# First x tile by TensorE, key softmax sums without transposes, memory features in five chunks

## The chip, the cores and the metric

One core of a Trainium2 chip. The time is device microseconds of one execution of the whole kernel. TensorE is PE, VectorE DVE, ScalarE ACT, GpSimd POOL, SyncE SP. SP computes nothing here; it issues nearly all DMAs, in order.

## The reference, cut to what matters

Two attention layers over the same x, mixed by a gate. 2048 tokens, 640 features, 32 heads of 20.

```python
g = sigmoid((x * gate_w).sum(-1))                 # per token
# A: linear attention with softmax features
q, k, v = split(x @ wqkv)
phi(t) = concat(softmax(t @ w_phi), softmax(-(t @ w_phi)))    # over 20, per head
o = (phi(q) @ (phi(k).T @ v)) / (phi(q) @ phi(k).sum(tokens) + 1e-6)
a = o @ wo
# B: four segments of 512 tokens; causal softmax inside one, a memory of those before
q, k, v = x @ wq, x @ wk, x @ wv
f(t) = where(t > 0, t + 1, exp(t))
for s in range(4):
    a_dot = softmax(causal(q_s @ k_s.T / sqrt(20))) @ v_s
    a_mem = (f(q_s) @ M) / (f(q_s) @ z + 1e-6)
    o_s = sigmoid(beta) * a_mem + (1 - sigmoid(beta)) * a_dot
    M, z = M + f(k_s).T @ v_s, z + f(k_s).sum(tokens)
b = concat(o_s) @ wo
out = g * a + (1 - g) * b
```

## The kernel before

The program is first a list of operations, each with its engines, an assumed duration, what it reads and writes, and a priority (`pr`, smaller is sooner). A planner (`schedule`) then places them one by one: of those that can start about now it takes the one with the smallest `pr`, and for an operation that may run on two engines the engine that is free sooner. SBUF tiles come from small pools and PSUM banks from a common one, and an operation waits until its tile is free. The result is a fixed order for each of PE, ACT, DVE, POOL and SP, and `emit` writes it out with a semaphore wait in front of what needs one. On the chip each engine works through its list in order: whatever stands behind a waiting instruction waits too. The planner's durations are guesses written in the code (a transposing DMA of 640 columns holds SP for 1.0 us and lands 2.0 us later).

`setup` loads x transposed into `xT` in four tiles of 512 tokens, by DMA from SP (`xload`), the first one ahead of everything. Three weights come through ACT's queue, the others through SP's. Wq and Wk of B are loaded as they are (`stq`, `stk`) and copied into `WB` with columns in a new order (L655, L657): each of five chunks of 128 columns holds four heads of 20, each followed by 12 of the 240 columns of the last twelve heads. Wk and Wq of A are loaded transposed (`wkT`, `wqT`) and multiplied with w_phi on PE (`fuse`).

B, for each segment n: `b_proj` makes `qk` in five chunks (L722). The 12-column remainders are written to `scr` in memory and read back (`relw`, `relr`) as groups 5 to 7 of `qk`, so that there are eight groups of four heads, each head on its own 32 partitions. `b_step`, for each group: QK on PE (L854), exp on ACT (L864, L883), the causal mask on POOL (L869, one instruction per block of 128 keys), PV on PE (L909); there are two exp buffers. From segment 1 on PE also reads out the memory (L912) with `b_pq`'s features (L825, L826, L828, four parts of two groups), and `combine` (L932 to L958) divides, scales and adds on DVE. `b_mem`, after segments 0 to 2: eight DMA transposes of the keys (`kT`, into `pk`), features (L784, L786, L788), 32 matmuls (L798), and the sum masked to the four heads' own blocks (L811).

A, keys: `a_k` for each of 16 tiles of 128 tokens, spread among B's steps by `AK`: pkA and vA on PE (L996, L997), two exps of 640 columns into `E` (L1003). For the softmax sums per head, `spread` transposes `E` by two DMAs, PE multiplies the result with a head mask (Zk, L1017), DVE takes the reciprocal (L1022) and normalizes `E` (L1023); `spread` transposes the normalized `E` again, and DVE adds that up over tokens into `acc` (L1032). After four tiles `a_kv` multiplies `E` with v (L1055) and adds to `KVZacc` (L1066).

A, queries: `a_q` for each segment, placed by `AQ`. `final` (placed by `FI`) multiplies the transposed results of both layers with `Wo` and stores the output. Results of all segments but the last are transposed by DMA (`oTB`, `oTA`), those of the last by PE.

## Time and profile before

| | |
|---|---|
| median of 3 runs (lowest to highest) | 391.79 us (388.26 to 394.04) |
| the profiled execution, and its span | 390.8 us, 388.9 us |
| busy: PE, ACT, DVE, POOL | 323.3, 268.1, 222.4, 106.3 us |
| mean granted TensorE clock | 0.925 |
| DMA packets, bytes | 97721, 33.97 MB |

How to read it: the span is from the first to the last instruction, the profiled execution's own time is taken around it. Busy time of PE includes matmuls at the lower clock; the granted clock is 1 where PE has its full 2.4 GHz and 0.5 where it has 1.2. Issuing a DMA isn't counted as busy, so SP's load shows only in its timeline.

### The profile page before, as it was taken

Reading aid. Unit: us, or ns where it says so; the run is one execution under the profiler, and the core shown is the slowest. Engines: PE = TensorE matmul, PEld = TensorE weight load, DVE = VectorE, ACT = ScalarE, POOL = GpSimd, SP = SyncE. Lnnn points to the kernel's source line nnn. Section 1 sums busy time; section 2 is a strip of 40 time slices with the busy share of each in tenths; the row PEclk is TensorE's granted clock in tenths of the full one; section 3 lists DMA queues with packets and bytes.
Section 4 is the critical chain, followed back from the end, with each engine's and each line's share of the span. In section 5 each row is a group of like instructions: output and inputs, shape, how many; then the busy total and the mean of one; then the engine's idle time right before and its main releaser. Section 6 shows DMA issues by size and latency. Waiting matters only on the chain.

```text
span 388.9 us, 9141 instructions
## 1 busy us (share of the span) xinstructions
PE 323.3 (83%) x3892; PEld 184.5 (47%) x3892; DVE 222.4 (57%) x447; ACT 268.1 (69%) x349; POOL 106.3 (27%) x155
## 2 busy tenths in 40 slices
PE   0997477996977989879976889899999897996786
PEld 0344144464543554446543545466555544552563
DVE  2203237985627577477818896777455476335760
ACT  2458545975865885847885879978697789567532
POOL 8402210232320122312323352512233323224210
PEclk9999868999995998969996999999999999996699
DMA  9999766366453666853452882023233513210002
GB/s 176 259 202 190 140 96 104 63 85 92 88 92 76 98 117 106 133 101 54 76 99 42 201 136 52 3 45 70 76 35 35 92 47 32 55 52 1 2 2 69
DMA packets 97721, 33.97 MB, mean 87 GB/s; under 512 B 89809, under 2 KB 95761, under 8 KB 97681
## 3 DMA queue, kind: packets, MB, share of 16 engines
q1 hardware_dynamic: 95616, 30.89, 44.4%
q10 hardware_dynamic: 1968, 2.46, 2.5%
q8 instruction: 31, 0.51, 0.6%
q0 software_dynamic: 96, 0.04, 0.1%
q14 instruction: 10, 0.07, 0.1%
HBM read 6.92 MB, written 4.59 MB: 30 GB/s over the span
## 4 chain that ended last, share of the span: by engine, by line
PE 47%; SPq 15%; ACT 14%; DVE 11%; DMA 7%; issue 2%; POOL 2%
SPq L598 13%; PE ps L1210 9%; ACT expT L864 7%; PE ps L722 7%; PE ps L996 5%; PE ps L909 5%; PE ps L854 4%; DMA TT<-E 3%; PE ps L1109 3%; PE ps L1211 2%; DVE cb L955 2%; DMA wkT<-in_A_wqkv_dram 2%; PE ps L1170 2%; SPq L603 2%; POOL expT L869 2%
## 5 line engine op out<-in xcount | busy, mean ns | idle before, releaser
L869 POOL TENSOR_SCALAR_AFFINE_SELECT expT<-expT 128x512 bf16<-128x512 bf16 x128 | 89.9, 705 | 260.2 <-ACT expT L864 203.5
L864 ACT ACTIVATE expT<-ps 128x1024 bf16<-128x1024 f32 x128 | 123.5, 1025 | 24.5 <-PE ps L854 24.4
L722 PE MATMUL ps<-xT,WB 128*128 128x512 bf16 x200 | 55.3, 423 | 10.6 <-DMA xT<-in_A_x_dram 10.6
L909 PE MATMUL ps<-v1B,expT 128*128 128x21 bf16 x1280 | 43.4, 174 | 6.0 <-DVE oA L1179 2.3
L909 PEld LDWEIGHTS ps<-v1B,expT 128*128 128x128 bf16 x1280 | 39.7, 97 | 17.2 <-POOL expT L869 6.9
L883 ACT ACTIVATE expT<-ps 128x1024 bf16<-128x1024 f32 x32 | 32.8, 1026 | 19.1 <-PE ps L854 19.0
L854 PE MATMUL ps<-qk 20*128 20x384 bf16 (+3 forms) x512 | 36.4, 320 | 10.9 <-DVE cb L955 5.2
L722 PEld LDWEIGHTS ps<-xT,WB 128*128 128x128 bf16 x200 | 19.1, 105 | 34.9 <-issue 19.6
L996 PE MATMUL ps<-WkA,xT 128*128 128x512 bf16 x80 | 26.5, 417 | 2.5 <-ACT qk L706 1.4
L743 PE MATMUL ps<-WvB,xT 128*128 128x512 bf16 x80 | 25.1, 396 | 3.9 <-DVE vA L707 3.7
L1003 ACT ACTIVATE E<-ps 128x640 bf16<-128x640 f32 x32 | 22.8, 711 | 8.0 <-PE ps L997 7.6
L706 ACT ACTIVATE out<-ps 128x640 bf16<-128x640 f32 x16 | 11.3, 704 | 22.5 <-PE ps L1211 19.6
L996 PE MATMUL ps<-WvA,xT 128*128 128x512 bf16 x80 | 25.6, 405 | 1.0 <-ACT E L1003 0.4
L1210 PE MATMUL ps<-Wo,oTA 128*128 128x512 bf16 x80 | 24.8, 396 | 1.7 <-ACT expT L864 1.7
L854 PEld LDWEIGHTS ps<-qk 20*128 20x128 bf16 x512 | 10.5, 93 | 32.8 <-issue 10.1
L1032 DVE TENSOR_TENSOR acc<-acc,TT 128x640 bf16<-128x640 bf16 x31 | 16.8, 541 | 15.0 <-DMA TT<-E 14.5
L1109 PE MATMUL ps<-xT,WqA 128*128 128x512 bf16 x100 | 24.3, 380 | 1.1 <-DVE cb L955 1.0
L706 ACT ACTIVATE qk<-ps 128x512 bf16<-128x512 f32 x29 | 17.2, 602 | 11.0 <-PE ps L722 10.5
L1023 DVE TENSOR_TENSOR E<-E,z 128x1280 bf16<-128x1280 bf16 x16 | 24.1, 1508 | 0.6
L1114 ACT ACTIVATE ET<-ps 128x512 bf16<-128x512 f32 x40 | 23.1, 607 | 1.9 <-PE ps L1109 1.2
L1210 PE MATMUL ps<-Wo,oTB 128*128 128x512 bf16 x80 | 23.7, 383 | 0.0
L955 DVE TENSOR_TENSOR cb<-ps,cs 128x640 bf16<-128x640 f32 x24 | 19.8, 825 | 0.8
(124 smaller groups left out, 551.4 us busy)
## 6 DMA issues: line engine op xcount, KB each, us to landing
out_dram<-out SPq DMA_DIRECT2D x16, 160.0 KB, 3.8
scr<-qk SPq DMA_DIRECT2D x16, 120.0 KB
qk<-scr SPq DMA_DIRECT2D x16, 120.0 KB
TT<-E SPq DMA_TRANSPOSE x64, 2.7
stq<-in_B_wq_dram ACTq DMA_DIRECT2D x1, 800.0 KB, 4.8
stk<-in_B_wk_dram ACTq DMA_DIRECT2D x1, 800.0 KB, 6.8
WvB<-in_B_wv_dram ACTq DMA_DIRECT2D x1, 800.0 KB, 11.8
WvA<-in_A_wqkv_dram SPq DMA_DIRECT2D x1, 800.0 KB
```

Of the source, the lines that this page charges most:

```text
L598: return e.dma_start_transpose(o() if callable(o) else o, i() if callable(i) else i)
L706: return e.activation(o(), i(), ACT.Copy)
L722: r = e.matmul(self.pf(pt, 0, 0, LSEG), lhsT=self.WB[:, w, kc, 128 * c:128 * (c + 1)], rhs=xT[:, kc, LSEG * n:LSEG * (n + 1)], start=(kc = ...
L854: r = e.matmul(self.pf(pts[i][0], pts[i][1], c0, N), lhsT=qk[32 * i:32 * i + DH, g, 1, 128 * j:128 * (j + 1)], rhs=qk[32 * i:32 * i + DH, ...
L864: self.op("act", d_act(1024), lambda e, p=p, pt=pt: e.activation(ex[:, 2 * p:2 * p + 2, off:off + 512], self.pbanks(pt, 0, 2, 512), ACT.Ex ...
L869: self.op("pool", d_pool(n_el), lambda e: e.affine_select(view(), view(), pattern=pat, compare_op=ALU.is_ge, fill=0.0, base=0, channel_mul ...
L883: return e.activation(ex[:, :, 1024:1280].rearrange("p (k b) c -> p k b c", k=2), src, ACT.Exp, scale=scale)
L909: r = e.matmul(self.pf(ad, b, 84 * q2 + 21 * i, 21) if n else self.pf(ad, 0, 84 * qi + 21 * i, 21), lhsT=ex[:, i, c0:c0 + 128], rhs=vt[:, ...
L955: self.op("dve", d_dve(640, 1, True), lambda e: e.tensor_tensor(cb[:, :, :, :].rearrange("p b t (x d) -> p b (t x) d", d=DH), Uv()[:, :, : ...
L996: e.matmul(self.pf(pt, 0, 0, 512), lhsT=l, rhs=W[:, kc, 0:512], start=(kc == 0), stop=(kc == 4))
L1109: r = e.matmul(self.pf(pt, 0, 0, LSEG), lhsT=self.WqA[:, kc, 128 * c:128 * (c + 1)], rhs=xT[:, kc, LSEG * S:LSEG * (S + 1)], start=(kc == ...
L1210: e.matmul(self.pf(pt, 0, 0, 512), lhsT=l, rhs=self.Wo[:, c, 0:512], start=(c == 0), stop=(c == 9))
```

## The change

The first x tile is loaded as it is, in one plain DMA (`xr`, in the second exp buffer's place), transposed by 20 PE operations against the identity and evacuated by DVE or ACT. The weights that ACT issued are issued by SP after it, Wq and Wk in two pieces each, and the copies into `WB` go by pieces; the order of the other loads on SP is new. ACT starts with an exp on a zeroed tile. The two zeroing memsets of `qk` on POOL are gone.

The last twelve heads are regrouped (`head_of`), so that groups 5 to 7 hold heads 20 to 31 in order. The memory works on the five chunks instead of the eight groups: five key transposes, features of 5 x 128 columns, 40 matmuls with a bigger block mask `Mm` (built by 22 POOL selections); query features are made by chunk (five operations of 512 columns for four of 1024), and the read-out of a group whose heads lie in several chunks takes one matmul per chunk (`mem_parts`).

In `a_k` the sums per head are made from `E` itself: 640 pairs are added into fp32, then 320 pairs, both on POOL or DVE, then DVE reduces five columns to one and takes the reciprocal. The transposes for Zk, Zk itself and its PSUM bank are gone; the remaining transpose of a tile is one DMA of 1280 columns for two of 640.

Planner numbers are new: durations of transposes (1.28 us and 1.5 us to landing; 2.3 and 1.6 for the 1280), `AK`, `AQ`, `FI`, priorities of key transposes and features.

```diff
+XH = tuple(20 + 48 * c // DH for c in range(NCH))
 
 
 def head_of(g, i):
-    return 4 * g + i if g < 5 else 20 + 3 * i + (g - 5)
+    return 4 * g + i
 
...
-    AK = (1.0, 1.05)
-    AQ = (18.2, 4.4)
-    FI = 9.0
+    AK = (1.6, 0.996)
+    AQ = (17.6, 4.1)
+    FI = 8.5
...
-        self.p_pq = self.pool(3, 2048)
-        self.p_tmp = self.pool(2, 2048)
-        self.p_pk = self.pool(1, 8192)
+        self.p_pq = self.pool(7, 1024)
+        self.p_pk = self.pool(1, 5120)
+        self.p_tmp = self.pool(2, 1280)
...
-            return self.dma("sp", xT[:, :, sl], x2d[sl, :], W=[(xT, s)], pr=pr, transpose=True, name=f"x{s}", dur=dur, lat=1.5)
-        x0 = xload(0, -40, 4.0)
-        sq = self.dma("act", self.stq[:, :, :], wsrc(ins["B_wq"]), W=[(self.stq, "*")], pr=-40, lat=5.0, name="stq")
-        sk = self.dma("act", self.stk[:, :, :], wsrc(ins["B_wk"]), W=[(self.stk, "*")], pr=-39, lat=5.0, name="stk", after=[sq])
-        sv = self.dma("act", self.WvB[:, :, 0:D], wsrc(ins["B_wv"]), W=[(self.WvB, "w")], pr=-38, lat=7.0, name="WvB", after=[sq])
-        self.dma("sp", self.wkT[:, :, :], wqkv[0:D, D:2 * D], W=[(self.wkT, "*")], pr=-38, dur=5.0, lat=1.5, transpose=True, name="wkT", after=[sk])
-        self.dma("sp", self.WvA[:, :, :], wsrc(wqkv[:, 2 * D:3 * D]), W=[(self.WvA, "*")], pr=-37, lat=6.0, name="WvA", after=[sv])
-        for i in range(1, SEG):
-            xload(i, -37 + i, 3.4)
-        self.dma("sp", self.wqT[:, :, :], wqkv[0:D, 0:D], W=[(self.wqT, "*")], pr=-30, dur=5.8, lat=1.5, transpose=True, name="wqT")
+            return self.dma("sp", xT[:, :, sl], x2d[sl, :], W=[(xT, s)], pr=pr, transpose=True, name=f"x{s}", dur=dur, lat=3.0)
+        zf = self.zf
+        self.op("dve", 0.1, lambda e: e.memset(zf[:, :, :], 0.0), W=[(zf, "*")], pr=-60)
+        self.op("act", 1.5, lambda e: e.activation(zf[:, :, :], zf[:, :, :], ACT.Exp), W=[(zf, "*")], pr=-60)
+        xr = self.xr
+        self.dma("sp", xr[:, :, :], x2d[0:LSEG, :].rearrange("(t p) d -> p t d", p=128), W=[(xr, "*")], pr=-60, lat=3.2, name="xr")
+        for k, (st, w) in enumerate(((self.stq, "B_wq"), (self.stk, "B_wk"))):
+            for h, (k0, k1) in enumerate(((0, 3), (3, 5))):
+                self.dma("sp", st[:, k0:k1, :], wsrc(ins[w])[:, k0:k1, :], W=[(st, h)], pr=-59 + 2 * k + h, lat=4.6 + 2.0 * k + h, name="st")
+        self.dma("sp", self.WvB[:, :, 0:D], wsrc(ins["B_wv"]), W=[(self.WvB, "w")], pr=-54, lat=8.0, name="WvB")
+        self.dma("sp", self.wkT[:, :, :], wqkv[0:D, D:2 * D], W=[(self.wkT, "*")], pr=-53, dur=5.0, lat=7.0, transpose=True, name="wkT")
+        self.dma("sp", self.WvA[:, :, :], wsrc(wqkv[:, 2 * D:3 * D]), W=[(self.WvA, "*")], pr=-52, lat=10.0, name="WvA")
+        xload(1, -51, 4.0)
+        xload(2, -50, 4.0)
+        self.dma("sp", self.wqT[:, :, :], wqkv[0:D, 0:D], W=[(self.wqT, "*")], pr=-49, dur=5.0, lat=2.5, transpose=True, name="wqT")
+        xload(3, -48, 4.0)
...
+        for s4 in range(4):
+            vx = lambda c0, c1, s4=s4: M3()[32 * s4:32 * s4 + 32, c0:c1, 1, :].rearrange("p c (i e) -> p c i e", e=21)
+            sel(lambda vx=vx: vx(0, NCH), [[0, NCH], [0, 4], [0, 21]], -DH, 1)
+            for c0, c1 in ((0, 3), (3, 5)):
+                f0 = 48 * c0 - DH * (XH[c0] - 20) + 12 * s4 - DH
+                assert all(48 * c - DH * (XH[c] - 20) == 48 * c0 - DH * (XH[c0] - 20) + 8 * (c - c0) for c in range(c0, c1))
+                v = lambda vx=vx, c0=c0, c1=c1: vx(c0, c1)
+                sel(v, [[8, c1 - c0], [-DH, 4], [0, 21]], f0, 1)
+                sel(v, [[-8, c1 - c0], [DH, 4], [0, 21]], DH - 1 - f0, -1)
         op("dve", 0.1, lambda e: e.memset(self.epsv[:, :, 0, :], 0.0), W=[(self.epsv, 0)], pr=-20)
...
-            op("pool", 2.5, lambda e, b=b: e.memset(self.qk[b][:, 5:8, :, :], 0.0), W=[(self.qk[b], f"r{i}") for i in range(4)], pr=-24 + b)
+        for c in range(NCH):
+            pt = self.pst("x0", 1)
+
+            def tr(e, c=c, pt=pt):
+                for tl in range(4):
+                    r = e.transpose(self.pb(pt, 0, 128 * tl, 128), xr[:, tl, 128 * c:128 * (c + 1)], idt[:, :])
+                return r
+            op("pe", 0.3, tr, R=[(xr, "*"), (idt, "*")], W=[(pt, 0)], pr=-30 + 0.1 * c, name="x0tr")
+            self.evac(512, lambda c=c: xT[:, c, 0:LSEG], lambda pt=pt: self.pb(pt, 0, 0, 512), W=[(pt, 0), (xT, (0, c))], pr=-30 + 0.1 * c, name="x0_ev", mode=2)
...
+            for h, (k0, k1) in enumerate(((0, 3), (3, 5))):
+                Wv = lambda w=w, k0=k0, k1=k1: self.WB[:, w, k0:k1, :].rearrange("p k (b r) -> p k b r", r=32)
+                op("dve", 0.24 * (k1 - k0), lambda e, Wv=Wv, st=st, k0=k0, k1=k1: e.tensor_copy(
+                    Wv()[:, :, :, 0:DH], st[:, k0:k1, 0:400].rearrange("p k (b r) -> p k b r", r=DH)), R=[(st, h)], W=[(self.WB, (w, 0, h))], pr=-31 + w, name="WBc")
...
-            self.dma("sp", qk[32 * i:32 * i + DH, 5:8, :, :].rearrange("p c w t -> p c (w t)"), scr.rearrange("(i m d) w t -> i d m (w t)", i=4, m=3)[i],
+            self.dma("sp", qk[32 * i:32 * i + DH, 5:8, :, :].rearrange("p c w t -> p c (w t)"), scr.rearrange("(m i d) w t -> i d m (w t)", i=4, m=3)[i],
...
-        pk = self.sbt("pk", [128, 4, 1024], BF16, self.p_pk)
-        for g in range(NG):
-            self.dma("sp", lambda g=g: pk[:, :, 128 * g:128 * (g + 1)], qk[:, g, 1, :], R=self.qk_key(n, g)[-1:] if g < 5 else self.qk_key(n, g),
-                     W=[(pk, g)], pr=8 * n + 5.5 + 0.05 * g, transpose=True, dur=0.8, lat=2.0, name="kT")
+        pk = self.sbt("pk", [128, 4, D], BF16, self.p_pk)
+        for c in range(NCH):
+            self.dma("sp", lambda c=c: pk[:, :, 128 * c:128 * (c + 1)], qk[:, c, 1, :], R=[(qk, (1, c))],
+                     W=[(pk, c)], pr=8 * n + 2.0 + 0.6 * c, transpose=True, dur=1.25, lat=1.4, name="kT")
         for tl in range(4):
-            pr = 8 * n + 6.0 + 0.2 * tl
-            tm = self.sbt("tmp", [128, 1024], BF16, self.p_tmp)
-            rg = [(pk, g) for g in range(NG)]
-            self.op("dve", 0.45, lambda e, tl=tl, tm=tm: e.tensor_scalar(tm[:, :], pk[:, tl, :], 1.0, 1.0, op0=ALU.add, op1=ALU.max),
+            pr = 8 * n + 5.6 + 0.3 * tl
+            tm = self.sbt("tmp", [128, D], BF16, self.p_tmp)
+            rg = [(pk, c) for c in range(NCH)]
+            self.op("dve", 0.3, lambda e, tl=tl, tm=tm: e.tensor_scalar(tm[:, :], pk[:, tl, :], 1.0, 1.0, op0=ALU.add, op1=ALU.max),
                     R=rg, W=[(tm, "*")], pr=pr, name="pkt1")
-            self.op("act", d_act(1024), lambda e, tl=tl: e.activation(pk[:, tl, :], pk[:, tl, :], ACT.Exp), R=[(tm, "*")],
+            self.op("act", d_act(D), lambda e, tl=tl: e.activation(pk[:, tl, :], pk[:, tl, :], ACT.Exp), R=[(tm, "*")],
                     W=[(pk, ("t", tl))], pr=pr, name="pkexp")
-            self.op("dve", 0.8, lambda e, tl=tl, tm=tm: e.tensor_tensor(pk[:, tl, :], pk[:, tl, :], tm[:, :], ALU.min),
...
-            for g in range(NG):
-                b, c0 = (0, 84 * g) if g < 6 else (1, 84 * (g - 6))
-                for tl in range(4):
-                    v = vt[:, tl, :, :]
-                    rhs = v[:, 4 * g:4 * g + 4, :] if g < 5 else v[:, 20 + g - 5:20 + g - 5 + 10:3, :]
-                    r = e.matmul(self.pf(mp, b, c0, 84), lhsT=pk[:, tl, 128 * g:128 * (g + 1)], rhs=rhs, start=(tl == 0), stop=(tl == 3))
+            for c in range(NCH):
+                b, c0 = (0, 168 * c) if c < 3 else (1, 168 * (c - 3))
+                for k, h0 in enumerate((4 * c, XH[c])):
+                    n4 = min(4, H - h0)
+                    for tl in range(4):
+                        r = e.matmul(self.pf(mp, b, c0 + 84 * k, 21 * n4), lhsT=pk[:, tl, 128 * c:128 * (c + 1)],
+                                     rhs=vt[:, tl, h0:h0 + n4, :], start=(tl == 0), stop=(tl == 3))
             return r
-        self.op("pe", 32 * 0.04, mm, R=[(pk, ("t", tl)) for tl in range(4)] + [(vt, tl) for tl in range(4)] + [(vt, "one")], W=[(mp, 0), (mp, 1)], pr=pr, name="Mmm")
+        self.op("pe", 40 * 0.04, mm, R=[(pk, ("t", tl)) for tl in range(4)] + [(vt, tl) for tl in range(4)] + [(vt, "one")], W=[(mp, 0), (mp, 1)], pr=pr, name="Mmm")
...
-        for part in range(4):
-            pq = self.sbt("pq", [128, 2, LSEG], BF16, self.p_pq)
-            tm = self.sbt("tmp", [128, 2, LSEG], BF16, self.p_tmp)
-            pr = 8 * n - 0.4 + 2 * part
-            gs = slice(2 * part, 2 * part + 2)
-            R = [k for g in (2 * part, 2 * part + 1) for k in (self.qk_key(n, g)[:1] if g < 5 else self.qk_key(n, g))]
-            self.op("act", d_act(1024), lambda e, pq=pq, gs=gs: e.activation(pq[:, :, :], qk[:, gs, 0, :], ACT.Exp), R=R, W=[(pq, "*")], pr=pr, claim=[tm], name="pqexp")
-            self.op("dve", d_dve(1024, 4), lambda e, tm=tm, gs=gs: e.tensor_scalar(tm[:, :, :], qk[:, gs, 0, :], 1.0, 1.0, op0=ALU.add, op1=ALU.max),
+        for c in range(NCH):
+            pq = self.sbt("pq", [128, LSEG], BF16, self.p_pq)
+            tm = self.sbt("tmp", [128, LSEG], BF16, self.p_tmp)
+            pr = 8 * n - 0.4 + c
+            R = [(qk, (0, c))]
+            self.op("act", d_act(512), lambda e, pq=pq, c=c: e.activation(pq[:, :], qk[:, c, 0, :], ACT.Exp), R=R, W=[(pq, "*")], pr=pr, claim=[tm], name="pqexp")
+            self.op("dve", 0.27, lambda e, tm=tm, c=c: e.tensor_scalar(tm[:, :], qk[:, c, 0, :], 1.0, 1.0, op0=ALU.add, op1=ALU.max),
                     R=R, W=[(tm, "*")], pr=pr, claim=[pq], name="pqt1")
-            self.op("dve", 0.75, lambda e, pq=pq, tm=tm: e.tensor_tensor(pq[:, :, :], pq[:, :, :], tm[:, :, :], ALU.min),
+            self.op("dve", 0.44, lambda e, pq=pq, tm=tm: e.tensor_tensor(pq[:, :], pq[:, :], tm[:, :], ALU.min),
                     R=[(tm, "*")], W=[(pq, "*")], pr=pr, name="pqmin")
-            self.pq[2 * part] = (pq, 0)
-            self.pq[2 * part + 1] = (pq, 1)
+            self.pq[c] = pq
+
+    def mem_parts(self, g):
+        if g < 5:
+            return [(g, 168 * g, 0, 4)]
+        out = []
+        for c in range(NCH):
+            lo, hi = 20 + 48 * c // DH, 20 + (48 * c + 47) // DH
+            a, b = max(lo, 4 * g), min(hi, 4 * g + 3)
+            if a <= b:
+                out.append((c, 168 * c + 84 + 21 * (a - XH[c]), a - 4 * g, b - a + 1))
+        return out
...
-                        r = e.matmul(self.pf(ad, b, 168 + 84 * q2, 84), lhsT=pqi[0][:, pqi[1], 128 * qi:128 * (qi + 1)],
-                                     rhs=self.Mzb[(n - 1) % 2][:, g, :], start=True, stop=True, skip_group_check=True)
+                        for k, (pq, m0, a, nh) in enumerate(parts):
+                            r = e.matmul(self.pf(ad, b, 168 + 84 * q2 + 21 * a, 21 * nh), lhsT=pq[:, 128 * qi:128 * (qi + 1)],
+                                         rhs=self.Mzb[(n - 1) % 2][:, m0:m0 + 21 * nh], start=(k == 0), stop=(k == len(parts) - 1), skip_group_check=True)
...
-        T1 = self.spread(E, pr)
-        zp = self.pst("Zk", 1)
-
-        def zmm(e):
-            first = True
-            for s in range(2):
-                for c, (lo, hi) in enumerate(HEADS_OF):
-                    r = e.matmul(self.pf(zp, 0, 32 * s + lo, hi - lo + 1), lhsT=T1[:, 5 * s + c, :], rhs=Mk[:, c, lo - HB[c]:hi + 1 - HB[c]],
-                                 start=first, stop=True, skip_group_check=True)
-                    first = False
-            return r
-        self.op("pe", 10 * 0.034, zmm, R=[(T1, 0), (T1, 1)] + [(Mk, c) for c in range(NCH)], W=[(zp, 0)], claim=[rz], pr=pr, name="Zk")
-        self.op("dve", 0.55, lambda e: e.reciprocal(rz[:, :], self.pf(zp, 0, 0, 64)), W=[(zp, 0), (rz, "*")], pr=pr, name="Zrec")
+        T2 = self.sbt("TT", [128, 2 * NCH, 128], BF16, self.p_TT)
+        self.TTs.append(T2)
+        hs = lambda: T2.t.ap().rearrange("p c f -> p (c f)").bitcast(FP32).rearrange("p (h d) -> p h d", d=10)
+        self.op(("pool", "dve"), {"pool": d_pool(640, 2), "dve": d_dve(640)}, lambda e: e.tensor_tensor(hs(), Ev()[:, :, 0:10], Ev()[:, :, 10:20], ALU.add),
+                R=[(E, 0), (E, 1)], W=[(T2, 0), (T2, 1)], pr=pr, name="Zsum1")
+        self.op(("pool", "dve"), {"pool": d_pool(320, 2), "dve": d_dve(320)}, lambda e: e.tensor_tensor(hs()[:, :, 0:5], hs()[:, :, 0:5], hs()[:, :, 5:10], ALU.add),
+                W=[(T2, 0), (T2, 1)], pr=pr, name="Zsum2")
+        self.op("dve", d_dve(320), lambda e: e.tensor_reduce(rz[:, :], hs()[:, :, 0:5], axis=AX.X, op=ALU.add),
+                W=[(T2, 0), (T2, 1), (rz, "*")], pr=pr, name="Zsum3")
+        self.op("dve", 0.5, lambda e: e.reciprocal(rz[:, :], rz[:, :]), W=[(rz, "*")], pr=pr, name="Zrec")
         self.op(("pool", "dve"), {"pool": d_pool(1280, 2), "dve": d_dve(1280)}, lambda e: e.tensor_tensor(
             Ev(), Ev(), rz[:, :].rearrange("p (h o) -> p h o", o=1).to_broadcast([128, 2 * H, DH]), ALU.mult),
             R=[(rz, "*")], W=[(E, 0), (E, 1)], pr=pr, name="Anorm")
-        T2 = self.spread(E, pr)
+        self.spread(E, T2, pr)
...
-    def spread(self, E, pr):
-        T = self.sbt("TT", [128, 2 * NCH, 128], BF16, self.p_TT)
-        self.TTs.append(T)
-        for s in range(2):
-            self.dma("sp", lambda s=s: T[:, 5 * s:5 * s + 5, :], lambda s=s: E[:, s, :], R=[(E, s)], W=[(T, s)], pr=pr, transpose=True,
-                     dur=1.0, lat=2.0, name="TT")
+    def spread(self, E, T, pr):
+        self.dma("sp", lambda: T[:, :, :], lambda: E[:, :, :].rearrange("p s n -> p (s n)"), R=[(E, 0), (E, 1)], W=[(T, 0), (T, 1)], pr=pr, transpose=True,
+                 dur=2.3, lat=1.6, name="TT")
```

## Rows read from the trace of the kernel before

**Rows 1.** Windows: stretch, length, busy us (instructions) per engine, granted clock, DMA share, GB/s.
```profile
0.00:30.00 30.00, 18.70 (x93) 8.63 (x94) 5.36 (x14) 12.87 (x22) 11.94 (x24) 1.00 1.03 216
...
30.00:230.00 200.00, 163.96 (x1939) 92.59 (x1937) 125.54 (x231) 139.84 (x180) 50.37 (x66) 0.90 0.59 103
...
230.00:350.00 120.00, 112.19 (x1518) 65.46 (x1510) 72.13 (x160) 97.23 (x129) 36.31 (x53) 0.99 0.28 51
...
210.00:250.00 40.00, 36.86 (x436) 19.84 (x435) 32.95 (x57) 34.85 (x48) 17.76 (x18) 0.97 0.48 96
```

**Rows 2.** The page's chain that ended last, by engine.
```profile
PE 47%; SPq 15%; ACT 14%; DVE 11%; DMA 7%; issue 2%; POOL 2%
```

**Rows 3.** SP's timeline: start, length, queue, line, operation, count.
```profile
0.81 21.61 SPq L598 DMA_TRANSPOSE xT<-in_A_x_dram  x4
...
104.22 11.29 SPq L598 DMA_TRANSPOSE pk<-qk  x8
...
115.55 21.75 SPq L598 DMA_TRANSPOSE TT<-E  x12
```

**Rows 4.** Line L598, transposing DMAs: issue time min/median/max in ns.
```profile
L598 SPq DMA_TRANSPOSE TT<-E x64: 1200/1276/3497, 46.7 to 223.3; - x64
...
L598 SPq DMA_TRANSPOSE pk<-qk x24: 1188/1267/2186, 37.7 to 199.7; - x24
```

**Rows 5.** PE's timeline, gaps: idle time before, and releaser, in brackets.
```profile
50.73 0.41 PE L1017 MATMUL ps<-Mk,TT 128*128 128x7 bf16 x10 [6.94 <-DMA TT<-E]
...
118.36 0.61 PE L743 MATMUL ps<-WvB,xT 128*128 128x512 bf16 x1 [3.67 <-DVE vA L707]
...
207.11 0.61 PE L854 MATMUL ps<-qk 20*128 20x384 bf16 x8 [4.86 <-DVE cb L955]
...
219.55 0.39 PE L1017 MATMUL ps<-Mk,TT 128*128 128x7 bf16 x10 [0.98 <-ACT pk L786]
```

**Rows 6.** Waits: engine and line, releaser, total us, times, longest.
```profile
DVE tmp L784 <- DMA pk<-qk: 16.6, 3, 7.4
...
DVE acc L1032 <- DMA TT<-E: 14.5, 7, 3.0
```

**Rows 7.** Windows: after the longest gap, and the first projections.
```profile
50.00:60.00 10.00, 8.69 (x69) 4.95 (x70) 4.83 (x8) 6.10 (x9) 1.14 (x1) 0.71 0.61 98
...
10.50:15.00 4.50, 4.41 (x11) 1.59 (x12) 1.77 (x2) 0.60 (x1) 3.26 (x5) 1.00 1.17 227
```

**Rows 8.** Timeline of the start, DVE and PE.
```profile
5.61 1.20 DVE L655 COPY WB<-stq 128x2000 bf16<-128x2000 bf16 x1 [2.57 <-DMA stq<-in_B_wq_dram]
...
10.59 8.70 PE L722 MATMUL ps<-xT,WB 128*128 128x512 bf16 x30 [10.59 <-DMA xT<-in_A_x_dram]
```

**Rows 9.** The page's DMA issues: count, size, us to landing.
```profile
stq<-in_B_wq_dram ACTq DMA_DIRECT2D x1, 800.0 KB, 4.8
```

**Rows 10.** Groups by shape: busy us, mean ns, idle before.
```profile
L825 ACT ACTIVATE pq<-qk 128x1024 bf16<-128x1024 bf16 x12 | 12.7, 1055 | 2.8 <-DMA qk<-scr 1.6 <-PE ps L912 1.3
...
L1032 DVE TENSOR_TENSOR acc<-acc,TT 128x640 bf16<-128x640 bf16 x31 | 16.8, 541 | 15.0 <-DMA TT<-E 14.5
...
L811 DVE TENSOR_TENSOR Mzb<-M,Mm 128x672 bf16<-128x672 f32 x2 | 1.7, 859 | 0.1
...
L811 POOL TENSOR_TENSOR Mzb<-M,Mm 128x672 bf16<-128x672 f32 x1 | 1.5, 1467 | 0.4 <-DVE M L809 0.4
...
L1072 DVE TENSOR_REDUCE zf<-acc 128x10 f32<-128x640 bf16 x1 | 0.8, 807 | 0.0
```

**Rows 11.** Lines L828 and L942: ns min/median/max.
```profile
L828 DVE TENSOR_TENSOR pq<-pq,tmp x12: 681/692/1115, 58.7 to 322.9; 128x1024 bf16<-128x1024 bf16 x12
...
L942 DVE TENSOR_TENSOR cs<-cs,cf x24: 191/193/1153, 152.9 to 375.0; 128x32 f32<-128x32 f32 x24
```

**Rows 12.** Timeline around 226 us, POOL and DVE.
```profile
226.11 1.54 POOL L1079 TENSOR_TENSOR KVZ<-KVZacc,Mk 128x800 bf16<-128x800 f32 x1 [1.93 <-DVE KVZacc L1066]
...
226.55 1.15 DVE L942 TENSOR_TENSOR cs<-cs,cf 128x32 f32<-128x32 f32 x1
```

More of the change, by code (lines that the diff above doesn't have):

```diff
@@ L709, in evac, with xk @@
         return op
+    def xk(self, n):
+        return [(self.xT, (0, c)) for c in range(NCH)] if n == 0 else [(self.xT, n)]
     def b_proj(self, n):
@@ L1111, in mm @@
                 return r
-            op("pe", d_mm(*[512] * 5), mm, R=[(self.WqA, ic) for ic in range(NCH)] + [(xT, S)], W=[(pt, 0)], claim=[ET], pr=pr + 0.3 * c, name="pqA")
+            op("pe", d_mm(*[512] * 5), mm, R=[(self.WqA, ic) for ic in range(NCH)] + self.xk(S), W=[(pt, 0)], claim=[ET], pr=pr + 0.3 * c, name="pqA")
             for s in (1, 0):
```

70 lines of the change are left out of this document (35 added, 35 removed).

## The prediction

> **What bounds the kernel now.** I read the windows first, cut where the work changes. The span is 388.9 us; PE is busy for 323.3 us of it. In the first 30 us PE waits and then runs the projections of segment 0. From 230 to 350 us PE is busy for 112.2 of 120 us at a granted clock of 0.99: there it is the bound. The stage from 30 to 230 us is different: PE 164.0, ACT 139.8, DVE 125.5 of 200 us, and a granted clock of 0.90. No engine is full, yet PE is idle for 36.0 us [rows 1]. What else runs there? The chain that ended last gives 15% to SP's queue and 7% to DMA, 22% of 388.9 us = 86 us together [rows 2]. SP's timeline shows why. The queue first issues four transposed x tiles in 21.6 us; the key transposes come in bursts of eight that hold it for 11.3 us; and the twelve softmax transposes behind one burst take until 137 us [rows 3]. A transpose holds the queue for some 1.27 us and the data land 2.7 us or more after that; there are 64 of E and 24 of the keys [rows 4], 64 x 1.276 + 24 x 1.267 = 112 us of one in-order queue in a stage of 200 us.
>
> So PE's gaps are to be read for what stood behind SP. Eight gaps of more than 0.3 us lie in front of Zk, whose operand is the transposed E: the first is 6.94 us, the last 0.98, together 15.4. Two more, 3.67 and 4.86 us, follow the two late key bursts: DVE waits for the transposed keys and holds back the PSUM banks that PE wants next [rows 5]. DVE's own waits say the same: 16.6 us for the keys, 14.5 us for the transposed E [rows 6]. Each long gap is paid a second time: after the 6.94 us the granted clock of the next 10 us is 0.71 [rows 7]. A mean of 0.90 over 200 us is 40 us at 1.2 GHz, 20 us of full-speed work lost if PE had been busy throughout, 16 us at its busy share of 0.82.
>
> **The change part by part.** The sum is made against the profiled execution, 390.8 us: the span and 1.9 us around it. The median of the three runs is 391.79, 1 us more.
>
> (a) Start. The first projection waits for the transposed x tile until 10.59 us, though the first half of the weight copy on DVE begins at 5.61; its 30 matmuls take 8.70 us, the first 11 of them 4.41, so 0.40 each against 0.23 for the other 19, 1.9 us lost [rows 7, 8]. Now x comes as a plain load. The nearest row is Wq's, 800 KB landing 4.8 us after its issue beside the x transpose [rows 9]; 640 KB first in the queue should be there by about 5 us. Then come 20 transposes and five evacuations, and the weights, which are now on SP behind x, so that six plain issues stand ahead of wkT on that queue. I estimate the first projection at 8.5 us, 2 us sooner, and 1 us from running the slow spell on the transposes. Bounds: 0, if the weights, sharing the engines with x, come no earlier than 10.6; 5 us, if everything is there at the 5.6 of the row. Value: -3. The 20 transposes lie in PE's idle time. The twenty-odd extra mask operations on POOL replace two long memsets and lie before the first softmax mask, where POOL has nothing else to do.
>
> (b) PE work. Zk goes: 160 matmuls, ten in 0.41 us [rows 5], 6.5 us. Packing in five chunks adds 8 matmuls to each of three memory updates, and 4 per query tile to the memory read-outs of segments 1 to 3 (12 parts where there were 8): 24 + 48 = 72, at the same 0.041 us 3 us, on the path in the full stage. Value: -3.5.
>
> (c) Stalls. SP's load in the stage falls: 32 of 64 softmax transposes vanish, the other 32 become 16 twice as long (40 us at the old price per byte), and 24 key transposes become 15 (19 us): 112 becomes 59 us. The key transposes are also issued earlier in the order, one by one, so that the others no longer stand behind a burst. The eight Zk gaps lose their waiter altogether; the two behind the keys lose most of their wait. That is 23.9 of the 36.0 us. Not all comes back, since PE then meets the next late thing: the exp on ACT, the PSUM evacuation. I take 16. Bounds: 5 (little more than the shorter gaps) and 29 (also the gaps where DVE waits for the second transposed E).
>
> (d) Clock. If gaps go, so does the half-speed time behind them: 16 us x 16/36 = 7, and 9 since the longest ones go. Bounds 3 and 14.
>
> (e) New work on DVE and POOL. Each of 16 key tiles now adds 640 and then 320 pairs, on POOL or DVE, reduces 320 on DVE and takes a reciprocal. POOL's nearest two-input row is 1.47 us for 672 columns, DVE's 0.86 us for the same in fp32 and 0.54 for 640 in bf16; a reduction of 640 took 0.81 us [rows 10]. So a tile costs POOL some 1.4 + 0.7 = 2.1 us, or DVE 1.2, and DVE 0.45 for the reduction. Against this the two-input operations on query and key features shrink: 1024 columns took 0.69 us in the middle case [rows 11]; twelve of 1024 become fifteen of 512, and twelve become twelve of 640; with the one-input ones beside them about 11 us of DVE go, of which about 8 in this stage. What counts is what POOL does to DVE: the scale operation of 32 columns takes 0.193 us in the middle case and took 1.15 beside POOL's 1.54 us addition, until that ended; the 1024-column one ranges from 0.69 to as much as 1.12 us, which I put down to the masks [rows 11, 12]. So up to 0.96 us of DVE may be lost per addition. I take +3 for the path. Bounds: -4 (DVE's relief counts, the holds fall into idle time) and +17, rival 1. The Trainium skill speaks against the step here: GPSIMD Engine Reference, section 1 (Specifications), says that its SBUF interfaces are shared with VectorE and contend with instructions that read two SBUF inputs; the rows above agree. By that rule alone rival 1 would be the outcome.
>
> (f) ACT loses at most 9 us (12 x 1.055 us of exp on queries become 15 halves, 12 on keys five eighths) [rows 10]. It is hidden by PE in the full stage, and I count it as nothing; if ACT set the pace, 2 us more. The tail after 350 us changes only in order: 0, and 3 either way.
>
> Sum: 390.8 - 3 - 3.5 - 16 - 9 + 3 = 362.3 us.
>
> **The rivals.**
>
> 1. DVE becomes the bound, since POOL holds it. Of 125.5 us DVE loses 8, gains 16 x 0.45 = 7, and is held for 32 additions x 0.8 = 26 us (0.8: between the 0.43 and 0.96 of the two rows, nearer to the true addition): 151 us. In its densest 40 us before, DVE was busy for 32.95, a share of 0.82 [rows 1]; at that share the stage takes 184 us, 16 less than now. With the start 390.8 - 16 - 3 = 372, and up to 382 if masks also wait. For it: the held rows. Against: POOL was busy for only 50 of the 200 us, and most of DVE's idle time is waiting for DMA, which shrinks. If the planner puts the sums on DVE instead, 16 x 1.2 = 19 us take the place of 26: 366.
>
> 2. The transfers were hidden anyway. Part of SP's time on the chain is the start-up, where the same bytes have to come in; in the stage PE may merely meet ACT and DVE instead of Zk. Then only (a) and (b) remain: 384, up to 392. Against: the gaps end on Zk and on the keys by name.
>
> 3. Nearly all comes back: (c) 29 and (d) 14, (a) 5, (e) 0: 390.8 - 5 - 3.5 - 43 = 339; I place the case at 338 to 350. The stage from 230 to 350 shows that this order of work can hold PE at 93%.
>
> 4. Slower: POOL's additions stand in its in-order queue ahead of the causal masks, PV waits for the mask, and the exp waits for its buffer, of which there are two. If each tile puts its 2.1 us and one hold of 0.9 on PE's path, it is 16 x 3 = 48 us against 31.5 gained: 390.8 + 16.5 = 407. It decides for slower by 2% from (31.5 + 9)/16 = 2.5 us per tile on. Against: three quarters of POOL's time in the stage is free [rows 1].
>
> **How the numbers follow.** Forecast (352 to 371) 0.58; rival 1 (371 to 382) 0.16; rival 2 (382 to 392) 0.11; rival 3 0.09; rival 4 0.06. The likeliest is 362. A range of 345 to 384 takes in the forecast, rival 1, 0.04 of rival 3 and 0.02 of rival 2: 0.80. The bounds of (c) alone move the sum by +11 and -13, those of (d) by +6 and -5, so the range is no wider than they make it. A change of 2%, 7.8 us, is about what a measurement can tell here, so faster means under 384: 0.58 + 0.16 + 0.09 + 0.02 of rival 2 = 0.85; same 0.10; slower 0.05.
>
> **What the changed profile would show.** (a): the first projection near 8.5 us, behind transposes. (b): PE about 3 us less busy at equal clock. (c): no wait of PE for a transposed E, DVE's waits for keys under 3 us, SP and DMA on the chain at 12% or less. (d): a clock over 0.95 in the stage. (e): DVE's two-input operations at 1 us or more beside POOL's additions; if these are a third of all, rival 1 holds. Wrong I would be, above all, if PE's idle time stayed near 36 us with other releasers, which the new order of all queues may bring: none of it can be read from this trace.

## The result, and the profile after

The changed kernel took **372.25 us** (median of 4 runs, 371.36 to 373.26) against 392.45 us (4 runs, 388.26 to 394.04) for the kernel before on the same chip: a ratio of 0.950, 95% interval 0.942 to 0.958. It is faster by 5%, 20 us, where the sum had 28.5; 372 lies inside the range and just outside the band of 352 to 371 that the forecast had to itself, at the lower edge of rival 1's.

The page's chain that ended last, by engine, after the change:

```profile
PE 47%; DVE 24%; ACT 12%; DMA 8%; SPq 5%; issue 2%; POOL 1%; DVEq 0%
```

SP's queue and DMA fell from 22% to 13% [rows 2]; DVE stands in their place, 24% for 11%. The windows of [rows 1], after:

```profile
0.00:30.00 30.00, 21.99 (x120) 11.15 (x121) 8.98 (x22) 14.33 (x27) 18.34 (x42) 1.00 0.98 235
30.00:230.00 200.00, 177.50 (x2084) 100.13 (x2085) 162.39 (x298) 161.11 (x218) 90.35 (x103) 0.92 0.41 72
230.00:350.00 120.00, 107.12 (x1459) 64.13 (x1458) 65.20 (x148) 84.70 (x109) 33.71 (x52) 0.94 0.25 45
```

In the stage PE is idle for 22.5 us, not 36.0. DVE has gone from 125.5 to 162.4 of 200 us, 81%. The clock has hardly recovered: 0.92 after 0.90. The stage from 230 to 350 us, in which the change touches only the query features, the read-outs and the order, lost 5 us of busy PE.

Fixed windows compare unlike work, since the key tiles now end sooner. So here are windows cut at the exp of the last key tile, at 213 us before:

```profile
30.00:213.00 183.00, 149.48 (x1740) 83.68 (x1739) 110.01 (x205) 126.48 (x164) 43.26 (x60) 0.89 0.57 97
213.00:388.90 175.90, 155.08 (x2065) 92.23 (x2063) 107.03 (x229) 128.78 (x165) 51.13 (x72) 0.95 0.28 56
```

and at 191 us after:

```profile
30.00:191.00 161.00, 141.45 (x1673) 81.09 (x1673) 128.85 (x232) 128.24 (x172) 74.78 (x86) 0.92 0.42 70
191.00:369.70 178.70, 157.74 (x2037) 92.74 (x2033) 105.73 (x230) 121.79 (x161) 49.27 (x69) 0.95 0.26 51
```

The key stage is 22 us shorter, the second half 2.8 us longer. And DVE does 19 us more in the shorter stage: a share of 0.60 has become 0.80. Who is late now? PE's timeline shows the longest gaps of the stage (idle time and releaser in brackets), which answer to [rows 5]:

```profile
48.79 0.29 PE L897 MATMUL ps<-qk 20*128 20x256 bf16 x4 [2.91 <-DVE WqA L738]
...
123.12 1.25 PE L756 MATMUL ps<-xT,WB 128*128 128x512 bf16 x5 [2.84 <-DVE oB L993]
...
163.94 0.61 PE L897 MATMUL ps<-qk 20*128 20x384 bf16 x8 [2.52 <-DVE cb L998]
```

No gap of the stage names a transpose any more. DVE's waits of [rows 6] are 3.4 and 1.4 us instead of 16.6 and 14.5:

```profile
DVE tmp L818 <- DMA pk<-qk: 3.4, 1, 3.4
...
DVE acc L1071 <- DMA TT<-E: 1.4, 4, 0.5
```

What held DVE is seen in the two timelines around the gap of 2.52 us. POOL:

```profile
160.62 2.35 POOL L1062 TENSOR_TENSOR E<-E,z 128x1280 bf16<-128x1280 bf16 x1 [0.62 <-DVE cs L976]
```

DVE, the scale of 32 columns and what follows it:

```profile
161.00 2.02 DVE L986 TENSOR_TENSOR cs<-cs,cf 128x32 f32<-128x32 f32 x1
163.06 0.82 DVE L998 TENSOR_TENSOR cb<-ps,cs 128x640 bf16<-128x640 f32 x1
```

The scale, 0.19 us in the middle case, begins while POOL multiplies E by its reciprocal and ends when POOL does; `cb`, for which PE waits, comes 2 us late. The gap of 2.84 us has the same cause: that multiplication at 118.62 us, and an accumulating addition beside it that took 2.61 us. It is not one of the additions that the change brings. It is the normalization of E, all 16 of which ran on DVE before; in the new plan two stand on POOL. (A fuller DVE is not what decides that: of the kernels below, e3 and e5, which have no new sums, put one there, and e4, which has them, none.) As in [rows 7], the gap is paid twice:

```profile
163.90:170.00 6.10, 6.06 (x45) 4.21 (x46) 4.15 (x10) 2.44 (x3) 1.27 (x2) 0.60 0.54 89
```

PE is busy throughout these 6 us, at a granted clock of 0.60.

### The profile page after: what moved, and what is told of

It is laid out like the page before. It is cut to its first block, busy times and chain, and to the rows that moved or that the text cites. A ratio compares the mean times of both kernels' runs of the same rounds, so it can differ in the third digit from the quotient of the medians.

```text
span 369.7 us, 8985 instructions
## 1 busy us (share of the span) xinstructions
PE 321.2 (87%) x3824; PEld 185.0 (50%) x3824; DVE 243.6 (66%) x482; ACT 264.4 (72%) x358; POOL 142.4 (39%) x197
## 4 chain that ended last, share of the span: by engine, by line
PE 47%; DVE 24%; ACT 12%; DMA 8%; SPq 5%; issue 2%; POOL 1%; DVEq 0%
PE ps L1246 10%; PE ps L756 9%; ACT expT L907 7%; PE ps L952 5%; PE ps L1145 4%; DMA TT<-E 4%; DVE acc L1071 4%; PE ps L777 3%; PE ps L897 3%; SPq L601 3%; DVE E L1062 3%; PE ps L1039 3%; PE ps L1247 2%; DMA stq<-in_B_wq_dram 2%; SPq L606 2%
## 5 line engine op out<-in xcount | busy, mean ns | idle before, releaser
L912 POOL TENSOR_SCALAR_AFFINE_SELECT expT<-expT 128x512 bf16<-128x512 bf16 x128 | 91.4, 716 | 182.4 <-ACT expT L907 146.0
L756 PE MATMUL ps<-xT,WB 128*128 128x512 bf16 x200 | 54.4, 418 | 6.6 <-DVE oB L993 2.8
L897 PE MATMUL ps<-qk 20*128 20x512 bf16 (+3 forms) x512 | 36.2, 316 | 10.5 <-DVE cb L998 4.6
L926 ACT ACTIVATE expT<-ps 128x1024 bf16<-128x1024 f32 x32 | 32.8, 1024 | 4.5 <-PE ps L897 4.3
L1039 PE MATMUL ps<-WkA,xT 128*128 128x512 bf16 x80 | 25.1, 400 | 1.7 <-DVE vA L738 1.7
L1145 PE MATMUL ps<-xT,WqA 128*128 128x512 bf16 x100 | 25.8, 403 | 0.6 <-DVE oA L1215 0.6
L1071 DVE TENSOR_TENSOR acc<-acc,TT 128x640 bf16<-128x640 bf16 x31 | 23.2, 748 | 2.1 <-DMA TT<-E 1.4
L1246 PE MATMUL ps<-Wo,oTB 128*128 128x512 bf16 x80 | 24.5, 392 | 0.0
L737 ACT ACTIVATE qk<-ps 128x512 bf16<-128x512 f32 x26 | 15.6, 599 | 11.5 <-PE ps L756 11.5
L1062 DVE TENSOR_TENSOR E<-E,z 128x1280 bf16<-128x1280 bf16 x14 | 21.0, 1503 | 0.5
L1212 DVE RECIPROCAL as<-ps 128x32 f32<-128x32 f32 x16 | 5.7, 355 | 23.6 <-PE ps L1206 23.6
```

The lines of the kernel that those rows point to most:

```text
L756: r = e.matmul(self.pf(pt, 0, 0, LSEG), lhsT=self.WB[:, w, kc, 128 * c:128 * (c + 1)], rhs=xT[:, kc, LSEG * n:LSEG * (n + 1)], start=(kc = ...
L897: r = e.matmul(self.pf(pts[i][0], pts[i][1], c0, N), lhsT=qk[32 * i:32 * i + DH, g, 1, 128 * j:128 * (j + 1)], rhs=qk[32 * i:32 * i + DH, ...
L912: self.op("pool", d_pool(n_el), lambda e: e.affine_select(view(), view(), pattern=pat, compare_op=ALU.is_ge, fill=0.0, base=0, channel_mul ...
L926: return e.activation(ex[:, :, 1024:1280].rearrange("p (k b) c -> p k b c", k=2), src, ACT.Exp, scale=scale)
L1039: e.matmul(self.pf(pt, 0, 0, 512), lhsT=l, rhs=W[:, kc, 0:512], start=(kc == 0), stop=(kc == 4))
L1062: self.op(("pool", "dve"), {"pool": d_pool(1280, 2), "dve": d_dve(1280)}, lambda e: e.tensor_tensor(Ev(), Ev(), rz[:, :].rearrange("p (h o ...
```

## The experiments

Two theories came from these rows. **T1:** DVE, fuller and held by POOL, is the new bound of the key stage, and that is where the missing 10 us are. **T2:** the order decides: what the key stage gains is given back in the second half unless the order of the rest is fitted to it. First the change was taken apart. Each ratio is to the kernel before on the same chip, with its 95% interval; the kernel after stands at 0.950.

**e1, the start alone:** of the diff only `xr`, its transposes, the loads and copies of the weights.

```diff
-        x0 = xload(0, -40, 4.0)
+        self.dma("sp", xr[:, :, :], x2d[0:LSEG, :].rearrange("(t p) d -> p t d", p=128), ...
```

> The kernel before with the start of the change alone: first x tile by PE, weights on SP by pieces, new order of loads. My theory: the start is a small part, since the changed kernel's first projection came at 9.95 us where it was 10.59; 0 to 3 us faster than before, so 389 to 393. Rival (the start carries the gain, as everything later only follows it): 8 us or more, under 385.

399.2 us, 1.012 (0.998 to 1.025): neither expectation, and not told from no change. This kernel keeps the two memsets of `qk` on POOL; in these runs their removal goes with the features. That matters at the start:

```profile
6.61 5.25 POOL L660 MEMSET qk<- 128x3072 bf16 x2
...
10.18 1.90 DVE L673 COPY WB<-stq 128x800 bf16<-128x800 bf16 x1 [0.99 <-DMA stq<-in_B_wq_dram]
...
12.14 6.97 PE L743 MATMUL ps<-xT,WB 128*128 128x512 bf16 x20 [4.09 <-DVE WB L673]
```

The copy of the second half of Wq ends at 12.08 us, just behind the memsets (11.86); without them it takes 0.37 to 0.64 us (after, e4, e7, e8, e11, e12). So the first projection comes 1.55 us later here than in the kernel before, and e1 is not the start as the changed kernel has it.

**e2, the key sums alone:** `a_k` as after, everything else as before.

```diff
-        T1 = self.spread(E, pr)
-        zp = self.pst("Zk", 1)
+        self.op(("pool", "dve"), {"pool": d_pool(640, 2), "dve": d_dve(640)}, ... name="Zsum1")
```

> The kernel before with the key softmax sums on POOL and DVE alone: no Zk, half the softmax transposes, key transposes still in bursts of eight. My theory: this part frees PE of Zk's gaps and carries most of the gain, 10 to 16 us faster, 376 to 383. Rival (DVE, held by POOL, pays it all back): within 4 us of before, 388 to 394.

394.2 us, 0.998 (0.992 to 1.004): what I expected fell. The time is the rival's, but not its reason, since the key stage did get shorter. PE's waits on transposed E are gone, and the last key exp comes at 198 us instead of 213. The windows, cut there, show where it went:

```profile
30.00:198.00 168.00, 141.20 (x1627) 79.17 (x1628) 132.15 (x230) 128.92 (x167) 73.74 (x80) 0.90 0.45 75
198.00:393.20 195.20, 162.44 (x2006) 95.15 (x2004) 111.31 (x236) 124.85 (x161) 45.18 (x68) 0.89 0.24 48
```

The key stage is 15 us shorter; the second half, in which no instruction was changed but the last tile's sums, is 19 us longer: 33 us of idle PE where there were 21, and a clock of 0.89 for 0.95.

**e3, the features alone:** five chunks, masks, `mem_parts`.

```diff
-        pk = self.sbt("pk", [128, 4, 1024], BF16, self.p_pk)
+        pk = self.sbt("pk", [128, 4, D], BF16, self.p_pk)
```

> The kernel before with the memory in five chunks alone: 15 key transposes issued one by one for 24 in bursts, smaller features. My theory: the two gaps behind the key bursts and some DVE time go, 4 to 9 us faster, 383 to 388. Rival (SP is still full with softmax transposes, so that what is taken out is filled by them): within 3 us of before.

389.3 us, 0.987 (0.977 to 0.997): a gain of some 5 us (1 to 9), the lower part of what was expected; the interval does not exclude the rival's 3 us.

**e4, all but the constants:**

```diff
-    AK = (1.6, 0.996)
-    AQ = (17.6, 4.1)
-    FI = 8.5
+    AK = (1.0, 1.05)
+    AQ = (18.2, 4.4)
+    FI = 9.0
```

> The changed kernel with the old planner numbers for where key and query tiles and the final products go (AK, AQ, FI as before). My theory: the removed work makes the gain, not the placement: 370 to 376. Rival (the new placement makes it): half of the 20 us or more goes back, 382 or more.

384.2 us, 0.975 (0.967 to 0.983), as the rival expected. So three numbers of the planner are worth 2.5% (give or take 1.2), some 10 us. Its key stage ends at 192 us, within 1 us of that of after; the second half is longer:

```profile
191.00:383.00 192.00, 164.98 (x2035) 97.35 (x2030) 107.49 (x239) 121.45 (x161) 44.66 (x66) 0.90 0.24 49
```

Between equal cuts it takes 192 us instead of 178.7, of which 7 are PE's busy time at a lower clock and 6 idle time. That speaks for T2.

**e5, the constants alone,** the diff of e4 turned round, on the kernel before.

> The kernel before with the three new priority constants (AK, AQ, FI) and nothing else of the change. In the kernel after these constants are worth 384.2 - 372.3 = 12 us. If they only fit the order to key sums that no longer wait on transposes, they are worth nothing here, where the key transposes still come late: 390 to 397 us, PE's waits on transposed E stay near 14 us. If the order is better whatever the sums are, 378 to 386 us.

393.8 us, 1.007 (1.003 to 1.011): they are no better order in themselves. PE waits for transposed E as long as expected, 13.6 us.

**e6, key sums and constants:** the diffs of e2 and e5 together.

> The kernel before with the new key sums and the new priority constants; x by DMA transposes and the memory features as before. The key sums alone gave 394.2. If the key stage that they shorten is only spent when the second half is laid out again for it, this one comes to 376 to 384. If the features and the start are what makes room (no part pays without the others), 388 to 395 us.

396.7 us, 1.013 (1.006 to 1.021). T2 as I had put it (fit the constants and the sums pay) fell: with the clock at 0.88 the second half took 190 us here too.

**e9, all but the start,** and **e10, all but the features:** the diffs of e1 and e3 turned round, on the kernel after.

> The kernel after with the start of before: the first x tile by DMA transpose, weights in one piece each, the loads on the queues of before. The key sums, the features and the new priority constants stay. The start brought PE's first projection only 0.64 us forward and alone measured +1.2%. If it is worth what that row shows, 370 to 376 us. If the parts pay only together (the loads of the start also set when the first key tiles can go, and with it the order of all that follows), 382 to 392.

379.1 us, 0.964 (0.956 to 0.972), between the two expectations.

> The kernel after with the memory features of before (2048 elements a piece, groups of 128 rows); start, key sums and new priority constants stay. Key sums and constants without features and start measured 396.7. If the features are what makes room on VectorE for the key sums (0.79 busy in the key stage without them), 386 to 396. If the start is what those two lacked, 372 to 380.

381.3 us, 0.971 (0.963 to 0.979), again between them. (The memsets are back in e10, and with them the late first projection, 12.13 us.) So added to sums and constants (e6, 1.013) the features bring 4.9% and the start 4.3%, though alone they are worth -1.3% and +1.2%; both together bring 6.3%. The parts one by one (e1, e2, e3, e5) add up to nothing, +0.3%; the whole is -5%. What the key sums are worth in the whole was not measured: the kernel after with the sums of before was not run.

**e7, one reduce** in the place of two additions and a reduce, on the kernel after:

```diff
-        self.op(("pool", "dve"), ... name="Zsum1")
-        self.op(("pool", "dve"), ... name="Zsum2")
-        self.op("dve", d_dve(320), lambda e: e.tensor_reduce(rz[:, :], hs()[:, :, 0:5], axis=AX.X, op=ALU.add), ...
+        self.op("dve", d_dve(1280), lambda e: e.tensor_reduce(rz[:, :], Ev(), axis=AX.X, op=ALU.add), ...
```

> The kernel after, each tile's key sums as one reduce of 1280 elements on VectorE instead of two halving additions (10 of 16 on GpSimd) and a reduce of 320. VectorE: estimated at 1.4 to 1.5 us a tile (480 ns for the reduce of 320 in after, four times the elements) instead of 1.0, so +7 us; GpSimd loses 17 us of adds. If GpSimd's adds hold VectorE (the accumulating adds 748 ns instead of 541), these come back to 600 ns or less, some -6 us, and the time is 369 to 374. If VectorE's own busy time decides alone, 374 to 378.

367.2 us, 0.937 (0.931 to 0.944): below both expectations, and faster than both kernels, by 5 us than the changed one (the two intervals just touch). POOL lost 24.6 us of additions, not the 17 expected. The reduce takes 1.476 us at the median, as estimated. Its stage, to be held against that of after:

```profile
30.00:230.00 200.00, 174.02 (x2163) 100.14 (x2161) 165.83 (x293) 168.47 (x229) 72.40 (x89) 0.97 0.41 74
```

79 more matmuls in less busy time: the clock is 0.97, not 0.92. PE is idle for 26 us, more than after, but behind PE's first instruction gaps of more than 1.5 us sum to 8.9 us in the whole span, against 15.3 after and 22.2 before. DVE is as busy as in after (165.8), so its busy share alone does not decide. Nor did the holds go away as I expected: the accumulating addition still takes 698 ns on average (748 after), beside masks and three normalizations on POOL.

**e8, no accumulation:** the 31 additions left out.

```diff
-                self.op("dve", 0.5, lambda e, h=h: e.tensor_tensor(acc[:, :, :], acc[:, :, :], T2[:, :, 64 * h:64 * h + 64], ALU.add), ...
```

> The kernel after without the 31 additions that accumulate the transposed E over the tokens (all but the first copy); the transposes stay. The sum over the tokens is that of one half tile. This takes 23.2 us from VectorE, nearly all of it in the key stage (VectorE 0.82 busy at 30 to 210 us), and no work from any other engine. If VectorE bounds the key stage, the last key exponential comes at about 180 instead of 191 us and the time is 358 to 365. If the second half gives back what the key stage gains, the last key exponential is earlier all the same, but the time is 368 to 373. If VectorE bounds nothing, both stay.

364.7 us, 0.933 (0.925 to 0.940). DVE is busy for 18 us less, 225.5 for 243.6, and the time is 1.8% (give or take 1.1), some 7 us, shorter; the last key exp comes at 186 us. That is 5 of the 11 us by which T1 had the exp sooner, with a time at the upper edge of T1's range: it speaks for T1 in kind.

**e11, a column of ones beside v.** It takes the token sum of E in fp32 on PE, not in bf16 on DVE.

```diff
-        v = self.sbt("vA", [128, D], BF16, self.p_vA)
+        v = self.sbt("vA", [128, H, 21], BF16, self.p_vA)
-        self.spread(E, T2, pr)
```

> The kernel after with a column of ones beside each head's 20 columns of v (128x32x21), so that the matmuls that sum E times v over the tokens give the sum of E as well: the 16 DMA transposes of E, the copy and the 31 accumulating additions on VectorE fall away, the matmuls get 168 instead of 160 columns, the accumulators of their sums too. Without the additions alone it was 364.7. If the transposes that are left there still cost something (DMA TT<-E stood with 4.1% on the chain of after), 354 to 362. If they were hidden by then, 363 to 367. Wider matmuls are estimated at 5% of those of 160 columns, under 2 us.

370.4 us, 0.943 (0.936 to 0.950): neither expectation. The 16 transposes are gone as well as the additions, and it is slower than e8 by 1.0%, about as much as the intervals can tell. DVE is as little busy as in e8 (225.1 us), yet the gain over after is 0.7%, within the noise; so e8's gain can't be put down to DVE's busy time alone. PE's longest waits in the stage are now for masks on POOL (4.5 us in 5) and for the `WqA` evacuation (4.1). Nothing here tells whether that is the wider matmuls or the order that the planner made of it.

**e12, the halving additions on DVE alone:**

```diff
-        self.op(("pool", "dve"), ... name="Zsum1")
+        self.op(("dve",), ... name="Zsum1")
```

and the same for `Zsum2`.

> The kernel after with the two halving additions of each tile's key sums on VectorE alone (22 of 32 ran on GpSimd). GpSimd loses 24.6 us of two-input adds; VectorE gains some 13 to 15 us (10 additions of 640 at under 890 ns and 12 of 320 at under 744 ns) less what GpSimd's adds held it. One reduce in their place measured 367.2. If that gain came from GpSimd's adds being gone (the holds, and the trip to GpSimd and back that the sums made), 364 to 370. If it came from VectorE having less to do for the sums than three instructions, 373 to 380.

374.5 us, 0.956 (0.949 to 0.963): the second expectation, as far as the intervals tell it from after's 0.950. Taking 24.6 us of additions off POOL brought nothing once DVE had to do them; the plan has four normalizations on POOL instead of two. The row of one of them:

```profile
146.39 2.47 POOL L1062 TENSOR_TENSOR E<-E,z 128x1280 bf16<-128x1280 bf16 x1 [3.72 <-DVE z L1061]
```

and what DVE did beside it, two additions that take 0.49 us each when nothing is beside them:

```profile
146.22 2.98 DVE L1071 TENSOR_TENSOR acc<-acc,TT 128x640 bf16<-128x640 bf16 x2
```

A gap of 1.84 us on PE ends at 151.46, behind a `vA` evacuation that stood later in DVE's queue.

## Why the prediction came out as it did

The direction was right, and PE's waits on transposes went as forecast; the size was not: 28.5 us forecast, 20.2 measured, 19.2 between the two profiled spans. Step by step:

**(a) Start, -3.** The first projection came 0.64 us sooner, not 2:

```profile
5.76 2.29 PE L679 MATMUL ps<-ident,xr 128*128 128x128 bf16 x20 [5.76 <-DMA xr<-in_A_x_dram]
9.95 7.04 PE L756 MATMUL ps<-xT,WB 128*128 128x512 bf16 x20 [1.89 <-ACT WB L688]
```

x was there at 5.76 us; ACT's copy of a weight half was late. Nor did the slow spell run off on the transposes: twelve of the 20 projections begin 0.43 us apart, ten of the 30 did before, and the others 0.22 in both. PE's idle time in the first 30 us fell by 3.3 us, but 2.3 of these are the transposes themselves. In the whole, the start is worth 1.4%, give or take 1.2 (0.964 without it, 0.950 with it), some 5 us; alone, in e1, it is worth none. I had not foreseen that a part's worth depends on the others.

**(b) PE work, -3.5.** The instructions are as counted (3892 - 160 + 72 + 20 = 3824). By the time from one matmul's start to the next, Zk took 4.7 us before, not 6.5, and the 72 new ones 2.0, so the step gave 2.7 us; the 20 transposes, 2.3 us, were counted nowhere, since they lie in idle time.

**(c) Stalls, -16.** PE's idle time in the stage fell by 13.5 us, and over the span by 17.1 (65.6 to 48.5). Both Zk and the keys have gone from its releasers. This step held in size, its remainder too: "PE then meets the next late thing", which is DVE. Two of its signs were narrowly missed: SP and DMA have 13% of the chain, not 12 or less, and DVE's waits for keys are 3.4 us, not under 3. And it read too much off the eight gaps: only three of them, 9.3 of the 15.4 us, name a transpose. (The 2.7 us to landing in its first paragraph count from the issue, not from the end of the hold.) Which part of the change took the idle time away is not shown, as the sums alone (e2) and with the constants (e6) gain nothing.

**(d) Clock, -9, over 0.95 in the stage. This step failed.** The clock is 0.92 there, and 0.94 instead of 0.99 from 230 to 350 us. (b) and (d) should have taken 12.5 us from PE's busy time; it fell by 2.1, from 323.3 to 321.2. The idle terms (a, c, e) were to give 16 us and gave 17. By the granted clock in the two traces, PE was busy at 1.2 GHz for 45.0 us before and for 40.6 after. Half of the difference, 2.2 us, is what the clock gave back, where 9 were forecast; that is 6.8 of the 9.3 us missing between the spans. I had the lost clock go with the gaps in proportion. It did not: in the stage, gaps of more than 1.5 us went from six of 22.2 us in sum to four of 10.0, but the time at 1.2 GHz only from 41.0 to 30.7 us. More than half of that, 17 us, begins behind gaps of 1.3 us or less; the longest stretch has one of 0.72 us 3 us ahead of it and one of 1.13 inside:

```profile
141.47:151.71 10.24, 8.93 (x37) 3.06 (x35) 9.76 (x20) 6.83 (x9) 2.54 (x4) 0.50 0.27 52
```

And from 230 to 350 us PE was busy at 1.2 GHz for 13.2 us, for 3.4 before. In e7 the long gaps of the stage are three of 5.0 us in sum, the clock of the stage is 0.97, and PE's busy time over the span is 313.7 us, 7.5 less than after, 5.5 of them by the clock (29.5 us at 1.2 GHz), while its idle time is 1.3 us more (49.8): most of e7's gain is the clock that (d) had promised.

**(e) New work, +3.** Mis-sized as well. The features gave DVE 5 us back, not 11: their additions became shorter in the middle case but were held more often (the one of 512 columns: 0.425 us at the median, 0.545 on average). DVE's busy time in the key stage rose by 19 us. The groups by shape (busy us, mean ns), to be read beside [rows 10, 11]:

```profile
L1071 DVE TENSOR_TENSOR acc<-acc,TT 128x640 bf16<-128x640 bf16 x31 | 23.2, 748 | 2.1 <-DMA TT<-E 1.4
...
L861 DVE TENSOR_TENSOR pq<-pq,tmp 128x512 bf16<-128x512 bf16 x15 | 8.1, 545 | 0.6 <-ACT pq L858 0.3
...
L1055 POOL TENSOR_TENSOR TT<-E 128x640 f32<-128x640 bf16 x10 | 13.9, 1390 | 4.1 <-ACT E L1046 4.1
...
L1057 POOL TENSOR_TENSOR TT<-TT 128x320 f32<-128x320 f32 x12 | 10.7, 894 | 2.5 <-DVE TT L1055 1.7
```

The same accumulating addition took 541 ns on average before. Rival 1 put DVE at a share of 0.82 and the time at 372 to 382; 0.80 and 372 were measured, so it holds in its result, but not by its sum, which had 26 us of holds by 32 additions. POOL got 22 of them. As an estimate, count for each DVE instruction with two inputs in SBUF what it took beyond the median of its kind with POOL idle: POOL cost DVE 17.7 us in the stage, 5.1 before; 7.2 of it beside the additions, 5.3 beside masks, 3.9 beside the two normalizations. Not a third of these instructions, but four of 147, were held for 1 us or more, the worst by the normalizations. (The POOL instruction of [rows 12], from which the prediction took its hold, is a multiplication, not an addition; and the 366 of rival 1 comes to 363 at its own share of 0.82.) That relieving DVE pays, as rival 1 says, has e8 for it and e11 not; moving the additions to DVE gains nothing (e12).

**(f) ACT** lost 3.7 us over the span, hidden. **Rivals 2 to 4:** the transfers were not hidden (DVE's 31 us of waits fell to 5); PE's waits on masks came to 2.6 us in the stage, far from the 48 of rival 4.

**What stays open.** Why the second half runs at a clock of 0.88 to 0.90 in e2, e4 and e6 and at 0.95 before and after: its instructions are the same, the order is not, and its idle time is spread over many waits of 0.3 to 3 us on ACT and DVE. With a new plan for every kernel, the order alone moves the time by some 10 us (e4), so the differences of 2 to 10 us between e7, e8, e11, e12 and after are not to be split further by cause. Why the clock falls behind short gaps, and stayed at 2.4 GHz behind one of 1.74 us at 108 us in after, no run tells. That the normalizations on POOL cost the gaps behind them is read from the rows; a kernel that only pins them to DVE was not tried (the plans of e4 and e11 leave all 16 on DVE and are not clearly faster, but differ in more). Nor was the kernel after without the key sums.
